# Turning the first group's input on the matrix engine: tails at once on column tiles, half loads, and the small first weights on ScalarE's queue

## The chip, the cores and the metric

The kernel runs on one core of a Trainium2 chip. The metric is the device time of one execution in microseconds (us). Times are medians of several executions. A "span" is the time from the first to the last instruction in one profiled execution; it is about 1.8 us shorter than the device time of the same execution. In the lines of the profile, PE stands for TensorE's matmuls and PEld for its weight loads, DVE for VectorE, ACT for ScalarE, POOL for GpSimd; SPq and ACTq are the issue of loads on SyncE's and on ScalarE's queue.

## The reference, cut to what matters

Six cross layers of a recommender network, 16384 rows of 416 features, bf16:

```python
B, F, D, L = 16384, 26, 16, 6          # Din = 416
def reference(x0, ws, bs):
    x = x0
    for l in range(L):
        proj = jnp.einsum('bd,de->be', x, ws[l]) + bs[l]
        x = x0 * proj + x
    return x
```

416 is 3 x 128 + 32. The last 32 features are the *tails*, and they are what makes the start of this kernel awkward.

## The kernel before: the parts that matter

The batch is cut into 8 groups of 2048 rows, and a group into 4 chunks of 512 rows. The kernel works on transposed data (features on partitions). Groups 1 and up are transposed by the DMA engines while they load. Group 0 cannot wait for that: its chunks are loaded as they are and turned on TensorE (a matmul against an identity matrix, into PSUM, the memory that matmuls write), then copied to SBUF (the memory that the engines work from) by ScalarE (ACT) and VectorE (DVE).

The program gives every engine a list of instructions of its own, in order. `add("sp", ...)` issues a DMA from SyncE, `add("act", ...)` with a `dma_start` issues one from ScalarE.

```python
# order of the loads on SyncE's queue
load_nat(0, 0, 2)                     # chunk 0, first half
load_nat(0, 2, KK)                    # chunk 0, second half
load_wm(0, "sp")                      # big weights of layer 0: 384 x 416
for j in range(1, NJ):
    load_nat(j, 0, KK)                # chunks 1, 2, 3
load_w3(0, "sp")                      # narrow weights of layer 0: 32 x 416, four copies
load_group(1, lambda: load_wm(1, "sp"))
# ... (cut)

def load_group(g, between=lambda: None):      # (cut)
    turn(0)                           # DMA-transposed load, features 0..127
    add("sp", lambda h: h.dma_start_transpose(Tb, x0[rows, D - P:D]), ...)   # last 128 features
    turn(1); turn(2)
    between()                         # big weights of layer 1
    for j in range(NJ):               # the group's tails: 32 rows out of Tb, to four places
        add("sp", lambda h: h.dma_start(x0s[s][q, XW:XW + CH], Tb[P - T32:P, j * CH:(j + 1) * CH]), ...)

def transposed_chunk(j):
    ba, bb = ((0, 1), (3, 0), (1, 3), (0, 1))[j]          # PSUM banks
    # ... (cut) 12 transposes of 128 x 128 for features 0..383 and
    #     4 more for features 288..415, of which only the last 32 are used;
    #     two ScalarE copies and two VectorE copies out of PSUM

def first_job():
    # ... (cut)
    keep_busy(8, 3)                   # dummy matmuls
    full(g, l, 0, ba, True, True, chunks=[0])             # 128-row matmuls, 3 a tile and chunk
    full(g, l, 1, bb, True, True, chunks=[0])
    transposed_chunk(1)
    transposed_chunk(2)
    full(g, l, 0, ba, True, True, chunks=[1])
    transposed_chunk(3)
    load_w3(1, "act")
    full(g, l, 1, bb, True, True, chunks=[1])
    full(g, l, 0, ba, True, True, chunks=[2, 3])
    rows32(g, l, 0, ba, False)        # the 32-row matmuls: tails times narrow weights
    # ... (cut)
```

**R0** is the start of the first 32-row matmuls (group 0). They need the tails and the *narrow weights*. **R1** is the start of the 32-row matmuls of group 1's first tile. They need *group 1's rows*, the four small moves at the end of `load_group`.

## Time and profile before

| | before |
|---|---|
| device time, 3 runs | 477.22 us (477.04 to 478.33) |
| profiled execution | 477.49 us, span 475.7 us |
| R0, R1 in that profile | 14.03, 22.78 us |

The page of the profile: busy time and share of the span of each engine, and further down the share of each engine in the chain of work that ended last.

```profile
PE 462.2 (97%) x3325; PEld 195.7 (41%) x3379; DVE 404.0 (85%) x696; ACT 342.4 (72%) x372; POOL 6.8 (1%) x15
...
PE 95%; issue 1%; DMA 1%; ACT 1%; DVE 1%; SPq 0%
```

TensorE is the limit: 95% of the last chain is PE. Next is the timeline of TensorE alone. Its columns are start, length (us), engine, source line, operation, output<-inputs, shapes, count, and in brackets how long the engine sat idle before and what ended that.

```profile
5.81 1.24 PE L456 MATMUL ps<-x,wm 128*128 128x512 bf16 x5 [0.25 <-ACT x L565]
7.92 1.07 PE L561 MATMUL ps<-ident,x 128*128 128x128 bf16 x16 [0.87 <-DMA x<-in_x_dram]
9.56 1.05 PE L561 MATMUL ps<-ident,x 128*128 128x128 bf16 x16 [0.57 <-DVE x L568]
10.45 0.81 PE L456 MATMUL ps<-x,wm 128*128 128x512 bf16 x3
11.10 1.06 PE L561 MATMUL ps<-ident,x 128*128 128x128 bf16 x16
12.21 1.89 PE L456 MATMUL ps<-x,wm 128*128 128x512 bf16 x8
14.03 0.40 PE L477 MATMUL ps<-x,w 32*128 32x512 bf16 x4
...
20.31 2.54 PE L456 MATMUL ps<-x,wm 128*128 128x512 bf16 x11 [0.16 <-issue]
22.78 0.61 PE L477 MATMUL ps<-x,w 32*128 32x512 bf16 x8
```

L456 are the 128-row matmuls, L561 the transposes, L477 the 32-row matmuls. TensorE waited for chunk 1 (0.87 us) and for chunk 2 (0.57 us; the profile names the VectorE copy, but chunk 2 landed at 9.42, at the same moment). A matmul record is missing here and there: six matmuls were issued in the first line and the first of them, at about 5.6, has no record. The ends of matmuls are modelled: counted at 216 ns from the start of the sixth (6.67), the gap before 7.92 is about 1 us.

SyncE's issue of loads, from the same timeline:

```profile
2.13 1.44 SPq L521 DMA_DIRECT2D x<-in_x_dram  x3
3.61 2.79 SPq L285 DMA_DIRECT2D w<-in_ws_dram  x4
6.44 4.11 SPq L292 DMA_TRANSPOSE x<-in_x_dram  x1
...
18.66 2.52 SPq L304 DMA_DIRECT2D x<-ost  x4
```

L285 are the four narrow weight loads, L292 and L297 the transposing loads of group 1, L304 the moves of its rows.

### The profile page before, as it was taken

The numbers are of one execution on the slowest core, as the hardware profiler recorded it, in microseconds if no ns is written. First come the engines' busy times: TensorE is split into PE (matmuls) and PEld (weight loads), VectorE is DVE, ScalarE is ACT, GpSimd is POOL, SyncE is SP. The second block draws the span as 40 slices with busy tenths as digits, with TensorE's granted clock in tenths as the row PEclk, the third lists the DMA queues.
The fourth block names the chain that finished last, engine by engine and source line by source line (L and its number), as shares of the span: only waits on it lengthen the run. The fifth ranks groups of instructions, "written<-read, shape, count | busy, mean of one in ns | idle before, by whom it ended". The sixth has DMA issues, their size and how long they took to land.

```text
span 475.7 us, 8355 instructions
## 1 busy us (share of the span) xinstructions
PE 462.2 (97%) x3325; PEld 195.7 (41%) x3379; DVE 404.0 (85%) x696; ACT 342.4 (72%) x372; POOL 6.8 (1%) x15
## 2 busy tenths in 40 slices
PE   7999999999999999999999999999999999999995
PEld 6344444444444444444444444434444444444442
DVE  2888888888888888898889869988888888888896
ACT  4677777777777777777777777777777777777785
POOL 1000000000000000000000000000000000000000
PEclk9999999999999999999999999999999999999999
DMA  8866950640002397369308940990000039025899
GB/s 223 181 150 137 190 113 1 142 81 1 28 7 44 63 228 158 76 139 244 84 21 195 208 108 9 178 279 2 1 10 25 4 64 242 15 45 117 227 155 288
DMA packets 138363, 53.31 MB, mean 112 GB/s; under 512 B 112330, under 2 KB 137428, under 8 KB 138324
## 3 DMA queue, kind: packets, MB, share of 16 engines
q1 hardware_dynamic: 137848, 52.46, 49.2%
q8 instruction: 26, 0.43, 0.4%
q10 hardware_dynamic: 476, 0.32, 0.2%
q14 instruction: 13, 0.11, 0.1%
HBM read 5.97 MB, written 13.63 MB: 41 GB/s over the span
## 4 chain that ended last, share of the span: by engine, by line
PE 95%; issue 1%; DMA 1%; ACT 1%; DVE 1%; SPq 0%
PE ps L456 77%; PE ps L477 7%; PE ps L497 6%; PE ps L798 2%; DMA x<-in_x_dram 1%; PE ps L471 1%; ACT tw L394 1%; PE ps L561 1%; PE ps L488 1%; DVE x L864 0%; PE ps L809 0%; ACT x L852 0%; DVE x L858 0%; PE ps L841 0%; SPq L521 0%
## 5 line engine op out<-in xcount | busy, mean ns | idle before, releaser
L394 ACT ACTIVATE tw<-ps,bias 128x1024 bf16<-128x1024 f32 (+1 forms) x295 | 299.8, 1071 | 119.8 <-PE ps L477 80.7
L456 PE MATMUL ps<-x,wm 128*128 128x512 bf16 x1638 | 371.7, 379 | 5.8 <-issue 3.7
L456 PEld LDWEIGHTS ps<-x,wm 128*128 128x128 bf16 x1692 | 158.9, 98 | 213.5 <-issue 27.9
L403 DVE TENSOR_TENSOR tw<-tw,x 128x1024 bf16<-128x1024 bf16 (+1 forms) x285 | 192.3, 682 | 52.8 <-ACT tw L394 52.4
L408 DVE TENSOR_TENSOR x<-tw,x 128x1024 bf16<-128x1024 bf16 (+1 forms) x285 | 183.0, 682 | 0.0
L477 PE MATMUL ps<-x,w 32*128 32x512 bf16 x512 | 39.2, 379 | 0.0
L497 PE MATMUL ps<-x,wm 128*32 128x512 bf16 x564 | 33.0, 380 | 0.0
L434 ACT ACTIVATE ts<-ps,bias 128x512 bf16<-128x512 f32 x47 | 28.8, 701 | 0.0
L438 DVE TENSOR_TENSOR x<-ts,x 128x512 bf16<-128x512 bf16 x47 | 18.6, 417 | 3.7 <-DMA x<-x 3.6
L497 PEld LDWEIGHTS ps<-x,wm 128*32 128x32 bf16 x564 | 13.8, 96 | 17.6 <-issue 5.3
L477 PEld LDWEIGHTS ps<-x,w 32*128 32x128 bf16 x512 | 7.8, 92 | 27.6 <-issue 27.1
L436 DVE TENSOR_TENSOR ts<-ts,x 128x512 bf16<-128x512 bf16 x47 | 18.5, 417 | 0.0
L666 POOL COPY ost<-ot 128x512 bf16<-128x512 bf16 x6 | 5.4, 898 | 423.7 <-DMA ot<-x 423.7
L798 PE MATMUL ps<-wm,x 128*128 128x416 bf16 x48 | 9.5, 340 | 0.0
L852 ACT ACTIVATE x<-ps 128x416 bf16<-128x416 f32 x16 | 7.7, 533 | 2.0 <-PE ps L798 1.9
L568 DVE COPY x<-ps 128x512 bf16<-128x512 bf16 x4 | 1.7, 424 | 8.7 <-PE ps L561 8.7
L565 ACT ACTIVATE x<-ps 128x512 bf16<-128x512 bf16 x8 | 4.3, 594 | 5.6 <-PE ps L561 5.6
L798 PEld LDWEIGHTS ps<-wm,x 128*128 128x128 bf16 x48 | 4.3, 98 | 4.2 <-issue 1.0
L561 PE MATMUL ps<-ident,x 128*128 128x128 bf16 x64 | 4.6, 226 | 1.4 <-DMA x<-in_x_dram 0.9
L858 DVE TENSOR_TENSOR x<-x,x 128x832 bf16<-128x832 bf16 (+1 forms) x10 | 5.0, 504 | 1.1 <-ACT x L852 1.1
L488 PE MATMUL ps<-x,w 32*32 32x512 bf16 x188 | 5.9, 374 | 0.0
L471 PE MATMUL ps<-x,w 32*32 32x512 bf16 x208 | 5.6, 385 | 0.0
(38 smaller groups left out, 35.7 us busy)
## 6 DMA issues: line engine op xcount, KB each, us to landing
out_dram<-ost SPq DMA_DIRECT2D x6, 1664.0 KB, 7.1
x<-in_x_dram SPq DMA_DIRECT2D x7, 416.0 KB, 8.0
x<-x SPq DMA_DIRECT2D x24, 96.0 KB, 2.2
wm<-in_ws_dram SPq DMA_DIRECT2D x6, 312.0 KB, 3.7
out_dram<-ost SPq DMA_DIRECT2D x2, 832.0 KB, 6.7
x<-x SPq DMA_DIRECT2D x22, 64.0 KB, 2.0
out_dram<-x SPq DMA_DIRECT2D x3, 416.0 KB, 3.6
x<-ost SPq DMA_DIRECT2D x28, 32.0 KB, 2.2
```

Of the source, the lines that this page charges most:

```text
L394: add("act", lambda h, a=a, w=w, b0=b0: h.activation(tw[r][:, a * CH:(a + w) * CH], psum[:, b0 * CH:(b0 + w) * CH], ACT_F.Identity, bias=b ...
L403: add("dve", lambda h, a=a, e=e: h.tensor_tensor(tw[r][:, a * CH:e * CH], tw[r][:, a * CH:e * CH], x0s[s0][:, i * GC + a * CH:i * GC + e * ...
L408: add("dve", lambda h, a=a, e=e: h.tensor_tensor(xs[so][:, i * GC + a * CH:i * GC + e * CH], tw[r][:, a * CH:e * CH], src(i, a, e), ALU.ad ...
L434: add("act", lambda h: h.activation(ts[r][:, :], bank(b), ACT_F.Identity, bias=bias[:, 3, l:l + 1], scale=1.0), reads=[("ps", b), "bias"], ...
L436: add("dve", lambda h: h.tensor_tensor(ts[r][:, :], ts[r][:, :], x03, ALU.mult), reads=[("ts", r)] + tok0, writes=[("ts", r)], release=True)
L438: add("dve", lambda h: h.tensor_tensor(x3s[so][:, :], ts[r][:, :], res, ALU.add), reads=[("ts", r)] + rtok, writes=[("x3", so), ("x3", so, ...
L456: add("pe", lambda h, t=t, j=j: h.matmul(bank(banks[j]), wm[l][:, t, ecols], src(t, j, j + 1), start=(first and t == 0), stop=(not first a ...
L471: add("pe", lambda h, q=q, j=j, r=r, c=c, o=o: h.matmul(psum[o, banks[j] * CH:(banks[j] + 1) * CH], w3[l][q, i * P + c * T32:i * P + (c + ...
L477: add("pe", lambda h, q=q, j=j, r=r: h.matmul(bank(banks[j]), w3[l][q, ecols], src[q, :], start=first, stop=not first, tile_position=(r * ...
L488: add("pe", lambda h, l=l, b=b, s3=s3, ri=ri, qi=qi, ro=ro, qo=qo: h.matmul(psum[qo, b * CH:(b + 1) * CH], w3[l][qi, NT * P:D], s3[qi, :], ...
L497: add("pe", lambda h, t=t, j=j, src=src, l=l, b=b, ro=ro, qo=qo: h.matmul(psum[qo, b * CH:(b + 1) * CH], wm[l][:, t, NT * P:D], src(t, j, ...
L798: add("pe", lambda h, t=t: h.matmul(bank(b, n=D), xcol(t, j, kk), wm[l][:, t, :], start=(first and t == 0), stop=(not first and t == NT - 1)),
```

## The change

The intent: turn all tails of group 0 at once, four side by side on column tiles of TensorE (strips of 128 x 32, each with a matmul of its own), instead of four full transposes in each chunk; load chunks 1 to 3 in halves so that the first half can be turned while the second is in flight; use separate pairs of PSUM banks; and take the four small narrow weight loads off SyncE's queue. The core of the diff:

```diff
     load_wm(0, "sp")
     for j in range(1, NJ):
-        load_nat(j, 0, KK)
-    load_w3(0, "sp")
+        load_nat(j, 0, 2)
+        load_nat(j, 2, KK)
     load_group(1, lambda: load_wm(1, "sp"))
@@ transposed_chunk
-        ba, bb = ((0, 1), (3, 0), (1, 3), (0, 1))[j]
+        ba, bb = ((0, 1), (3, 0), (6, 7), (0, 1))[j]
-        first = (0, P, 2 * P, D - P)
-        seq = [(t, k) for t in range(NT) for k in range(KK)]
         ... (cut)
-        q = slice(j * T32, (j + 1) * T32)
-        add("dve", lambda h: h.tensor_copy(x0s[s][q, XW:XW + CH], psum_t(bb)[P - T32:P, CH:2 * CH]),
-            reads=[("ps", bb)], writes=[("x03q", s, j)])
+        for k2 in (0, 2):                       # first half, then second half
+            for t in range(NT):
+                b, o = place[t]
+                for k in (k2, k2 + 1):
+                    ... (cut: one 128 x 128 transpose)
+    def transposed_tails(b):
+        for k in range(KK):
+            for j in range(NJ):
+                o = slice(j * T32, (j + 1) * T32)
+                add("pe", lambda h, j=j, k=k, o=o: h.matmul(
+                    psum_t(b)[o, CH + k * P:CH + (k + 1) * P], x0n[:, j, k, NT * P:D], ident[:, :],
+                    is_transpose=True, tile_position=(0, j * T32)), ... writes=[("ps", b)])
+        add("dve", lambda h: h.tensor_copy(x0s[s][:, XW:XW + CH], psum_t(b)[:, CH:2 * CH]), ...)
@@ first_job
-        keep_busy(8, 3)
+        load_w3(0, "act")
+        keep_busy(5, 3)
         full(g, l, 0, ba, True, True, chunks=[0])
         full(g, l, 1, bb, True, True, chunks=[0])
         transposed_chunk(1)
         transposed_chunk(2)
         full(g, l, 0, ba, True, True, chunks=[1])
+        full(g, l, 1, bb, True, True, chunks=[1])
         transposed_chunk(3)
+        transposed_tails(1)
         load_w3(1, "act")
-        full(g, l, 1, bb, True, True, chunks=[1])
         full(g, l, 0, ba, True, True, chunks=[2, 3])
```

More of the change, by code (lines that the diff above doesn't have):

```diff
@@ L549, in transposed_chunk @@
     def transposed_chunk(j):
-        ba, bb = ((0, 1), (3, 0), (1, 3), (0, 1))[j]
+        ba, bb = ((0, 1), (3, 0), (6, 7), (0, 1))[j]
         s = slot(0)
-        first = (0, P, 2 * P, D - P)
-        seq = [(t, k) for t in range(NT) for k in range(KK)]
-        if j == 0:
-            seq = [(t, k) for k2 in (0, 2) for t in range(NT) for k in (k2, k2 + 1)]
-        for n, (t, k) in enumerate(seq + [(NT, k) for k in range(KK)]):
-            if j == 0 and n == NT * 2:
-                keep_busy(2, 3)
-            b, o = (ba, t * CH) if t < 2 else (bb, (t - 2) * CH)
-            c = slice(o + k * P, o + (k + 1) * P)
-            add("pe", lambda h, t=t, k=k, b=b, c=c: h.transpose(
-                psum_t(b)[:, c], x0n[:, j, k, first[t]:first[t] + P], ident[:, :]),
-                reads=[("nat", j, k), x0_tok(nat, 0, 0), "ident"], writes=[("ps", b)])
@@ L564, in transposed_chunk @@
-        for t in range(2):
-            add("act", lambda h, t=t: h.activation(
-                x0s[s][:, cols(t, j)], psum_t(ba)[:, t * CH:(t + 1) * CH], ACT_F.Copy),
-                reads=[("ps", ba)], writes=[x0_tok(s, t, j)])
-        add("dve", lambda h: h.tensor_copy(x0s[s][:, cols(2, j)], psum_t(bb)[:, 0:CH]),
-            reads=[("ps", bb)], writes=[x0_tok(s, 2, j)])
-        q = slice(j * T32, (j + 1) * T32)
-        add("dve", lambda h: h.tensor_copy(x0s[s][q, XW:XW + CH], psum_t(bb)[P - T32:P, CH:2 * CH]),
-            reads=[("ps", bb)], writes=[("x03q", s, j)])
+        place = ((ba, 0), (bb, 0), (ba, CH)) if j == 0 else ((ba, 0), (ba, CH), (bb, 0))
@@ new lines, in transposed_chunk @@
+        for k2 in (0, 2):
+            for t in range(NT):
+                b, o = place[t]
+                for k in (k2, k2 + 1):
+                    c = slice(o + k * P, o + (k + 1) * P)
+                    add("pe", lambda h, t=t, k=k, b=b, c=c: h.transpose(
+                        psum_t(b)[:, c], x0n[:, j, k, t * P:(t + 1) * P], ident[:, :]),
+                        reads=[("nat", j, k), x0_tok(nat, 0, 0), "ident"], writes=[("ps", b)])
+            if j == 0 and k2 == 0:
+                keep_busy(2, 3)
@@ new lines, in transposed_chunk @@
+        for t in range(NT):
+            b, o = place[t]
+            dst, sp_ = x0s[s][:, cols(t, j)], psum_t(b)[:, o:o + CH]
+            kw = dict(reads=[("ps", b)], writes=[x0_tok(s, t, j)])
+            if b == bb:
+                add("dve", lambda h, dst=dst, sp_=sp_: h.tensor_copy(dst, sp_), **kw)
+            else:
+                add("act", lambda h, dst=dst, sp_=sp_: h.activation(dst, sp_, ACT_F.Copy), **kw)
+    def transposed_tails(b):
+        s = slot(0)
+        for k in range(KK):
[3 more added lines that the diff above has]
+                    psum_t(b)[o, CH + k * P:CH + (k + 1) * P], x0n[:, j, k, NT * P:D], ident[:, :],
+                    is_transpose=True, tile_position=(0, j * T32)),
+                    reads=[("nat", j, k), x0_tok(nat, 0, 0), "ident"], writes=[("ps", b)])
+        add("dve", lambda h: h.tensor_copy(x0s[s][:, XW:XW + CH], psum_t(b)[:, CH:2 * CH]),
+            reads=[("ps", b)], writes=x03_toks(s))
```

## The prediction

> **What bounds the kernel.** TensorE. The chain of waits puts 95% of the span on matmuls, and the granted clock is full. From 9.56 us to 460 us the timeline shows matmuls issued back to back (216 ns from one 512-column matmul to the next). Anything won before the first tile of group 1 (20.3 us) should therefore reach the end one for one, unless group 1's loads become the new limit. Only the first 20 us change.
>
> **The opening before** (timeline of TensorE, and landings of the loads): first matmuls of chunk 0 from 5.6 us, when the first weights land (5.46); idle 6.9 to 7.92, waiting for chunk 1 (landed 7.88); 16 transposes (56 ns each, 0.89 us); idle 8.83 to 9.56, waiting for chunk 2 (landed 9.42; the profile names the VectorE copy, which ends at the same time); 16 transposes; 3 matmuls; 16 transposes; 9 matmuls; the 32-row matmuls at 14.03. For chunks 1, 2 and 3, 15 of 16 DMA engines finish by 6.51, 7.55 and 8.77; one engine is 1.4 to 1.9 us late and sets the landing.
>
> **What the change does, costed.**
> 1. Each chunk loses 4 tail transposes: 16 x 56 ns = 0.89 us. But chunk 0's are hidden under the wait for the weights, and chunk 1's and part of 2's lie between DMA waits. About 0.4 us counts.
> 2. All tails as 16 column-tile transposes, four side by side. The Trainium skill ("TensorEngine Tiling (Array Packing)", Key Properties) says that tiles run in parallel and that a mode change drains TensorE; in this trace four column-tile matmuls start 3 ns apart and a mode change costs about 0.1 us. Estimate: 4 x 56 ns + 0.2 = 0.4 us added.
> 3. A new wait: the tails go into the bank that chunk 3's third block was just turned into, so they wait for its VectorE copy: 0.2 us to its start, 0.42 us copy, 0.1 us back: about 0.7 us of TensorE idle right before the tails. Before, chunk 3's copies hid behind matmuls.
> 4. Half loads: first halves turn before the second halves land; after each landing 6 transposes (0.33 us) remain instead of 16 (0.89). This wins about 0.5 us after chunk 1 and again about as much after chunk 2, but the second only replaces the first where the late engine still sets chunk 2's landing.
> 5. Four narrow weight loads leave SyncE's queue (2.8 us of issue), three more chunk loads join (1.4 us): group 1's transposing loads are issued about 1.4 us earlier, but queue behind the same chunk bytes. ScalarE now issues the four (about 1.7 to 2.6 us from 5.6 us), which may delay its copies of chunk 1 until about 8.2 us.
> 6. Bank 3 no longer joins chunks 1 and 2: nothing measurable. VectorE saves three 0.43 us copies: off the path.
>
> **Sum.** If one engine is late again: -0.5 (halves) -0.4 + 0.4 (tails) + 0.7 (bank wait) = about +0.2 us. If it is not: both DMA idles (1.7 us) mostly vanish, less ScalarE's issue delay: about -1 us. Weighted: -0.5 us.
>
> Predicted **476.7 us**, range **475.6 to 477.8**. Chances: faster by over 2% 0.003, within 2% 0.992, slower by over 2% 0.005.
>
> **Right or wrong in the profile:** chunk 2's transposes follow chunk 1's with a gap under 0.4 us; 48 full transposes; 16 tail transposes within 0.5 us; a TensorE gap of 0.6 to 0.8 us just before them, ended by the VectorE copy; first 32-row matmuls between 12.9 and 14.4 us (before 14.03); from there the same stream, shifted by a constant.
>
> **What would make it wrong:** ScalarE's issue of the weights blocking its copies longer than 2.6 us; group 1's rows landing late (21.97 before, used at 22.77), capping the gain; the late engine moving.

## More of the kernel before

When a load has landed is read from its completions, 16 for each load: the trace has the time of each of them. The narrow weights (64 completions) had landed at 11.18 us, long before R0. Group 1's rows (64 completions) had landed at 22.53, a quarter of a microsecond before R1.

## The result

Ratios here and below are the mean time of one kernel's fast runs over the mean of the other's fast runs of the same rounds, so they are not quite the ratio of the medians that are quoted.

| | before | changed |
|---|---|---|
| device time | 477.31 us (476.76 to 478.33, 6 runs) | 477.80 us (477.39 to 478.82, 6 runs) |
| ratio | | 1.0011, 95% interval 0.9996 to 1.0026 |
| span of the profiled execution | 475.69 us | 476.40 us |
| R0, R1 | 14.03, 22.78 us | 14.76, 23.51 us |
| narrow weights landed | 11.18 us | 14.62 us |
| group 1's rows landed | 22.53 us | 23.15 us |

The interval reaches from just below 1 upward: the same within 2%, and no gain. The page of the profile after, the same lines:

```profile
PE 462.5 (97%) x3322; PEld 195.7 (41%) x3376; DVE 402.0 (84%) x693; ACT 342.1 (72%) x372; POOL 7.3 (2%) x15
...
PE 94%; DMA 2%; ACT 1%; issue 1%; DVE 1%; ACTq 0%; POOL 0%; POOLq 0%
```

The timeline of TensorE after, as shown for before (L558 are now the full transposes, L578 the tails on column tiles):

```profile
5.87 1.72 PE L456 MATMUL ps<-x,wm 128*128 128x512 bf16 x5
7.42 1.17 PE L558 MATMUL ps<-ident,x 128*128 128x128 bf16 x18
8.84 0.51 PE L558 MATMUL ps<-ident,x 128*128 128x128 bf16 x6 [0.25 <-DMA x<-in_x_dram]
9.19 1.46 PE L456 MATMUL ps<-x,wm 128*128 128x512 bf16 x6
10.48 0.83 PE L558 MATMUL ps<-ident,x 128*128 128x128 bf16 x12
11.83 0.41 PE L578 MATMUL ps<-ident,x 128*32 128x128 bf16 x16 [0.52 <-DVE x L568]
12.40 1.24 PE L456 MATMUL ps<-x,wm 128*128 128x512 bf16 x5 [0.16 <-ACT x L570]
14.76 0.40 PE L477 MATMUL ps<-x,w 32*128 32x512 bf16 x4 [1.11 <-DMA w<-in_ws_dram]
...
21.04 2.54 PE L456 MATMUL ps<-x,wm 128*128 128x512 bf16 x11 [0.16 <-issue]
23.51 0.61 PE L477 MATMUL ps<-x,w 32*128 32x512 bf16 x8
```

Nearly everything that was intended happened. The transposes of chunks 1 and 2 follow each other, with 0.25 us of idle before the last six. The 16 tail transposes take 0.41 us. The last 128-row matmul before R0 started at 13.26, and in the kernel before the step from there to the 32-row matmuls was 0.31 us: R0 could have been at 13.58, that is 0.45 us *earlier* than before. Then TensorE waited. R0 came at 14.76, and the releaser is `DMA w<-in_ws_dram`: the narrow weights. In the chain of waits after, this is one piece, which starts with the last of the four loads' issue and ends at 14.62 (start, length, what):

```profile
6.70 7.92 DMA w<-in_ws_dram
```

And SyncE's issue after:

```profile
2.45 2.86 SPq L521 DMA_DIRECT2D x<-in_x_dram  x6
5.35 4.52 SPq L292 DMA_TRANSPOSE x<-in_x_dram  x1
...
19.39 2.51 SPq L304 DMA_DIRECT2D x<-ost  x4
```

Group 1's first transposing load is issued 1.1 us earlier (5.35, before 6.44). Yet it landed later: 14.82 us against 13.81. Its issue alone took 4.52 us.

### The profile page after: what moved, and what is told of

The parts are those of the page before. It is cut to its first block, busy times and chain, and to the rows that moved or that the text cites. A ratio compares the mean times of both kernels' runs of the same rounds, so it can differ in the third digit from the quotient of the medians.

```text
span 476.4 us, 8347 instructions
## 1 busy us (share of the span) xinstructions
PE 462.5 (97%) x3322; PEld 195.7 (41%) x3376; DVE 402.0 (84%) x693; ACT 342.1 (72%) x372; POOL 7.3 (2%) x15
## 4 chain that ended last, share of the span: by engine, by line
PE 94%; DMA 2%; ACT 1%; issue 1%; DVE 1%; ACTq 0%; POOL 0%; POOLq 0%
PE ps L456 76%; PE ps L477 7%; PE ps L497 6%; DMA w<-in_ws_dram 2%; PE ps L811 2%; PE ps L471 1%; ACT tw L394 1%; PE ps L541 1%; PE ps L488 1%; DVE x L877 0%; PE ps L558 0%; PE ps L822 0%; ACT x L865 0%; ACT x L570 0%; DVE x L871 0%
## 5 line engine op out<-in xcount | busy, mean ns | idle before, releaser
L877 DVE TENSOR_TENSOR x<-x,x 128x832 bf16<-128x832 bf16 x8 | 4.6, 586 | 0.4 <-DMA x<-x 0.4
```

## The experiments

Seventeen runs were made, some of them of the same kernel on another occasion. All gave correct results. Each was timed in five rounds beside the kernel before. This table has for each profiled execution what the argument needs; it is worked out from the traces (landing: the last of 64 completions).

| run | narrow weights landed | R0 | rows landed | R1 | span | span - R1 |
|---|---|---|---|---|---|---|
| before | 11.18 | 14.03 | 22.53 | 22.78 | 475.69 | 452.91 |
| changed | 14.62 | 14.76 | 23.15 | 23.51 | 476.40 | 452.89 |
| w3_on_sync | 10.47 | 13.21 | 21.95 | 22.00 | 474.90 | 452.90 |
| w3_early_scalar | 6.61 | 16.19 | 22.46 | 24.94 | 477.83 | 452.89 |
| before_w3_scalar | 14.94 | 15.08 | 23.77 | 23.83 | 476.75 | 452.92 |
| whole_chunks | 14.45 | 14.58 | 23.17 | 23.33 | 476.24 | 452.90 |
| tails_bank7 | 13.96 | 14.01 | 22.33 | 22.76 | 475.66 | 452.90 |
| w3_sync_bank7 | 11.14 | 12.77 | 22.31 | 22.35 | 475.25 | 452.90 |
| w3_sync_whole_chunks | 11.21 | 14.26 | 22.41 | 23.01 | 476.07 | 453.06 |
| group1_rows_early | 10.94 | 12.58 | 21.35 | 21.40 | 474.30 | 452.90 |
| before_rows_early | 10.44 | 13.26 | 20.84 | 22.01 | 474.92 | 452.91 |
| w3_early_kept_busy | 6.83 | 14.85 | 21.76 | 23.60 | 476.50 | 452.90 |
| group1_rows_again | 11.27 | 13.67 | 21.98 | 22.42 | 475.33 | 452.91 |
| transposes_wait_w3 | 9.95 | 13.25 | 23.75 | 23.80 | 476.70 | 452.90 |
| changed_again | 14.15 | 14.29 | 23.01 | 23.06 | 475.96 | 452.90 |
| w3_on_sync_again | 11.25 | 13.58 | 22.95 | 23.00 | 475.99 | 452.99 |
| fastest_third | 11.28 | 12.65 | 21.91 | 21.95 | 474.85 | 452.90 |
| rows_early_w3_scalar | 14.26 | 14.30 | 21.98 | 23.05 | 475.94 | 452.89 |

Read the last column first. From R1 to the end every profiled execution took 452.9 us, within 0.2 us. So the whole case is decided by when R1 starts, and R1 starts when two things have come: TensorE has got there (8.75 us after R0, where nothing stops it), and group 1's rows have landed. The missing run, rows_early_only, had its profile in a throttled execution and is told below.

The theories. **Queue theory**: what cost is the wait for the narrow weights, which sit in ScalarE's queue and share the DMA engines with group 1's transposing loads. Rivals: the **halves theory** (twice as many chunk loads make everything behind them late), the **bank theory** (the wait before the tails, which the prediction had counted), and later the **limit theory** (group 1's rows).

### w3_on_sync

```diff
-        load_w3(0, "act")                 # in first_job
+    load_w3(0, "sp")                      # after the chunk loads, before load_group(1)
```

> The changed kernel with one part undone: the four narrow weight loads are issued by SyncE again, after the chunk loads and before group 1's transposing loads. Queue theory (the 1.1 us wait before the first 32-row matmuls exists because these loads sit in ScalarE's queue and share the DMA engines with group 1's transposing loads): they land before 11.8 us, the wait is gone, the first 32-row matmul starts at 13.5 to 13.8 us instead of 14.76, and the time is 0.2 to 0.5 us below the kernel before (about 1 us below the changed kernel), unless group 1's rows then land too late and cap it. Halves theory (twice as many chunk loads stretch the loading, so whatever is queued behind lands late): a wait of over 0.5 us stays before the 32-row matmuls and the time stays 0.3 us or more above the kernel before.

Measured: 477.35 us (476.71 to 477.66, 5 runs); before 477.14 us (476.71 to 477.98, 11 runs); ratio 1.0001, 0.9989 to 1.0013. The weights landed at 10.47, the wait was gone, and R0 came at 13.21. The profiled execution was also the fastest of the five. The median did not fall below the kernel before, so the expected time was missed. The queue theory was right about the wait, but something else stood behind it: the rows landed at 21.95 and were used at 22.00, with nothing to spare.

### w3_early_scalar

```diff
+    load_w3(0, "act")                     # before the loads of chunk 0
     load_nat(0, 0, 2)
@@ first_job
-        load_w3(0, "act")
```

> The changed kernel with the narrow weight loads still on ScalarE's queue, but issued right after ScalarE's first dummy activation (about 2.8 us) instead of about 5.4 us. Queue theory, sharpened: not the queue itself is at fault but sharing the engines with the transposing loads; issued early they land before 8.5 us, the first 32-row matmul starts at 13.5 to 14.0 us and the time is 0.1 to 0.6 us below the kernel before. If ScalarE's queue as such is slow: they land after 12 us again and the wait stays.

Measured: 477.65 us (476.73 to 479.64, 6 runs); before as above; ratio 1.0016, 0.9998 to 1.0033. The issue began at 1.4 us rather than at 2.8. The weights landed at 6.61, so ScalarE's queue is not slow as such. But the big first weights then landed at 7.01 (5.73 in the changed kernel), and something new happened. The timeline of TensorE shows six matmuls that took 2.70 us:

```profile
7.15 2.70 PE L456 MATMUL ps<-x,wm 128*128 128x512 bf16 x6 [1.82 <-DMA wm<-in_ws_dram]
```

and the window from 7.0 to 9.6 us (columns: window, its length, then busy time and count of PE, PEld, DVE, ACT and POOL, then the granted TensorE clock, the DMA share and GB/s) has a granted clock of 0.54:

```profile
7.00:9.60 2.60, 2.45 (x6) 0.89 (x7) 0.00 (x0) 0.00 (x0) 0.00 (x0) 0.54 1.41 291
```

The trace's own record has the full clock from 3.79 to 7.21 and half of it from 7.21 to 10.62. The halving followed 1.8 us of idle (5.33 to 7.15), and matmuls came every 427 ns instead of 216. That is one profile. The six runs, from 476.73 to 479.64, spread by 2.9 us. As a test of the queue theory the time of this run is inconclusive.

### before_w3_scalar

```diff
-    load_w3(0, "sp")                      # the kernel before, with this one part of the change
@@ first_job
+        load_w3(0, "act")
         keep_busy(8, 3)
```

> The kernel before with this one part of the change: the narrow first weights on ScalarE's queue. Queue theory: they land at 13.5 to 15 us, the first 32-row matmul (14.03 before) waits for them and starts at 14.3 to 15.2 us; time 0.3 to 1.1 us above the kernel before. Halves theory: whole chunk loads leave room, the weights land before 13 us and the time equals the kernel before within 0.2 us.

Measured: 478.25 us (477.71 to 479.03, 5 runs); before 477.14 us; ratio 1.0021, 1.0008 to 1.0034. This one part, alone, makes the kernel before slower. The timeline of TensorE in this run shows the same wait as in the changed kernel, with whole chunk loads and without the tails' change:

```profile
11.96 2.10 PE L456 MATMUL ps<-x,wm 128*128 128x512 bf16 x9
15.08 0.40 PE L477 MATMUL ps<-x,w 32*128 32x512 bf16 x4 [1.01 <-DMA w<-in_ws_dram]
```

The halves theory fell here.

### whole_chunks

```diff
     for j in range(1, NJ):
-        load_nat(j, 0, 2)
-        load_nat(j, 2, KK)
+        load_nat(j, 0, KK)
```

> The changed kernel with whole chunk loads (three loads instead of six), all else changed. Queue theory: the wait for the narrow weights stays (first 32-row matmul after 14.4 us), time 0.3 to 1.0 us above the kernel before; the idle between the transposes of chunks 1 and 2 grows because each chunk is waited for whole. Halves theory: the weights land before 13 us, no wait over 0.3 us, and the time is at or below the kernel before.

Measured: 477.70 us (477.33 to 478.21, 5 runs); ratio 1.0012, 1.0000 to 1.0024. The narrow weights landed at 14.45 and R0 was at 14.58: with or without halves, the weights set R0.

### tails_bank7

```diff
-        transposed_tails(1)
+        transposed_tails(7)
```

> The changed kernel with the tails turned into bank 7 instead of bank 1, so that they need not wait for the VectorE copy out of bank 1. My prediction called that wait 0.7 us of loss (the trace after shows 0.5 us of idle). If the narrow weights' landing is what ends last before the 32-row matmuls (queue theory), the 0.5 us only moves into the wait for them: the idle before the tails falls under 0.2 us, the wait before the first 32-row matmul grows from 1.1 to about 1.6 us, that matmul still starts after 14.4 us and the time stays within 0.2 us of the changed kernel. Bank theory (the bank wait eats the gain): the time falls by 0.4 to 0.6 us against the changed kernel, to about the kernel before.

Measured: 477.61 us (477.20 to 478.23, 5 runs); before 477.21 us (476.54 to 477.45, 9 runs); ratio 1.0014, 1.0001 to 1.0026. The wait before the tails was gone and the time did not move against the changed kernel (477.80). R0 was released by the weights at 13.96. They landed 0.66 us earlier than in the changed kernel's profile, so two expected numbers were missed: R0 came at 14.01, not after 14.4, and the wait for the weights did not grow. The bank wait was real, but it was not what set R0, so the bank theory fell.

### w3_sync_bank7

```diff
-        load_w3(0, "act")
+    load_w3(0, "sp")                      # as in w3_on_sync
-        transposed_tails(1)
+        transposed_tails(7)
```

> Narrow weights on SyncE again and the tails in bank 7. The first 32-row matmul starts about 0.5 us earlier than with the weights on SyncE alone (13.2 in that profile), at about 12.7. Limit theory (group 1's rows, which landed at 21.95 and were used at 22.00 there, are the next limit): TensorE then waits 0.3 to 0.6 us for those rows before the 32-row matmuls of group 1's first tile, and the time falls by at most 0.2 us, to 0.1 to 0.5 us below the kernel before. Without that limit: the whole 0.5 us arrives.

Measured: 477.19 us (477.00 to 477.39, 5 runs); before 477.21 us; ratio 1.0004, 0.9990 to 1.0018. R0 came at 12.77, 1.26 us earlier than in the profile before. R1 came only 0.42 us earlier. TensorE's timeline shows where the rest stayed:

```profile
12.77 0.40 PE L477 MATMUL ps<-x,w 32*128 32x512 bf16 x4
...
22.35 0.61 PE L477 MATMUL ps<-x,w 32*128 32x512 bf16 x8 [0.64 <-DMA x<-ost]
```

The 32-row matmuls of group 1 waited for `DMA x<-ost`, the rows, which landed at 22.31. This is the limit theory as expected, only that the time didn't even fall to 0.1 us below the kernel before.

### w3_sync_whole_chunks

```diff
     load_wm(0, "sp")
     for j in range(1, NJ):
-        load_nat(j, 0, 2)
-        load_nat(j, 2, KK)
+        load_nat(j, 0, KK)                # with w3_on_sync's edit
```

> Narrow weights on SyncE again, whole chunk loads: what the halves alone are worth. If they pay as predicted (about 0.5 us per chunk waited for), the idle between chunk 1's and chunk 2's transposes comes back at 0.5 us or more and the time is 0.3 to 0.6 us above the version with halves. If halves only add packets and issues: equal or up to 0.3 us faster.

Measured: 477.61 us (476.75 to 478.06, 5 runs); before 477.21 us; ratio 1.0011, 0.9998 to 1.0024. TensorE idled again before chunk 1's transposes (0.2 us) and before chunk 2's (0.3 us), less than the expected 0.5. R0 was at 14.26, later than in either run of w3_on_sync (13.21 and 13.58). In time no value of the halves is shown: the ratio lies between those of the two runs of w3_on_sync (1.0001 and 1.0015).

### group1_rows_early, group1_rows_again and fastest_third

One kernel, run on three occasions. On top of w3_sync_bank7, group 1's rows are moved ahead of the big weights of layer 1, and the narrow weights of layer 1 go to SyncE after them, so that nothing shares the engines with the transposing loads:

```diff
         turn(2)
-        between()
         for j in range(NJ):
             ...                           # the four moves of the rows
+        between()
@@
-    load_group(1, lambda: load_wm(1, "sp"))
+    load_group(1, lambda: (load_wm(1, "sp"), load_w3(1, "sp")))
@@ first_job
-        load_w3(1, "act")
```

> As the version with weights on SyncE and tails in bank 7, and group 1's four row moves issued before the second big weight load, and the second narrow weights on SyncE after them instead of on ScalarE's queue, so that nothing shares the engines with group 1's transposing loads. Limit theory: group 1's rows land 1 us or more earlier (before 21 us), TensorE does not wait for them, and the time is 0.5 to 1.2 us below the kernel before. If it stays at the kernel before within 0.2 us, the limit lies elsewhere.

> The fastest version once more, for a second sample on another occasion: 0.5 to 1.2 us below the kernel before, ratio 0.9975 to 0.999.

> The fastest version a third time (first narrow weights on SyncE, tails in bank 7, group 1's row moves ahead, second narrow weights on SyncE): its two samples gave 0.9988 and 1.0000 of the kernel before. If it is really faster: 0.2 to 0.9 us below the kernel before. If the first sample was luck: within 0.15 us of it. In the profile TensorE waits neither for the narrow weights nor for group 1's rows.

| occasion | this kernel | before, same rounds | ratio |
|---|---|---|---|
| group1_rows_early | 476.32 us (475.99 to 476.99, 5 runs) | 477.21 us | 0.9988, 0.9975 to 1.0000 |
| group1_rows_again | 476.96 us (476.04 to 478.54, 6 runs) | 477.04 us | 1.0000, 0.9988 to 1.0012 |
| fastest_third | 476.67 us (476.59 to 476.96, 5 runs) | 476.97 us | 0.9996, 0.9982 to 1.0009 |

Its median was the lower one each time, by 0.89, 0.08 and 0.30 us, but two of three intervals hold 1 well inside and the third ends at it. The mean of the three ratios, 0.9995, would be about a quarter of a microsecond, and even that is not proven. In the first profile the rows landed at 21.35, not before 21 as expected, and were used at once. In the second profile the big first weights landed at 6.72 (5.44 in the first), which differs between executions of the same kernel; R0 was 1.09 us later too (13.67 against 12.58). In the third, R0 was at 12.65, the earliest but one, and the rows stopped TensorE once more, at 21.91:

```profile
12.65 0.39 PE L477 MATMUL ps<-x,w 32*128 32x512 bf16 x4
...
18.70 2.77 PE L456 MATMUL ps<-x,wm 128*128 128x512 bf16 x12
21.95 0.61 PE L477 MATMUL ps<-x,w 32*128 32x512 bf16 x8 [0.49 <-DMA x<-ost]
```

### rows_early_only

```diff
         turn(2)
-        between()
         ...
+        between()                         # with w3_sync_bank7's edits; w3 of layer 1 stays on ScalarE
```

> Weights on SyncE, tails in bank 7, group 1's row moves ahead of the second big weight load, but the second narrow weights still on ScalarE's queue beside group 1's transposing loads. If the order of the row moves alone lifted the limit: rows land before 21.8 us, at most 0.3 us of wait for them, time 0.4 to 0.9 us below the kernel before. If sharing with the second narrow weights also costs: transposing loads end 0.3 to 0.7 us later than in the fastest version and its time is 0.2 to 0.5 us above that one.

Measured: four fast runs between 476.92 and 477.38; before 477.04 us; ratio 1.0002, 0.9989 to 1.0015. The profile fell in an execution of 607.19 us with a granted clock of 0.754, so its times can't be compared with the others. That misses the expected 0.4 to 0.9 us below, but the full version in the same rounds (group1_rows_again, 1.0000) can't be told from it either. What moving the second narrow weights adds is not shown.

### before_rows_early

The kernel before with the edits of group1_rows_early to `load_group(1)` and `load_w3(1)`, and nothing of the change.

> The kernel before, with group 1's four row moves ahead of the second big weight load and the second narrow weights on SyncE: the last two steps of the fastest version so far, without anything of the change. If the change's own parts (halves, tails at once) are what was won there, once the two waits were taken away: TensorE reaches the 32-row matmuls at about 14 us as before, group 1's rows landing earlier is worth nothing there, and the time is within 0.3 us of the kernel before. If the gain came from group 1's loads alone: 0.6 to 1 us below it.

Measured: 477.18 us (476.72 to 477.32, 5 runs); before 477.04 us; ratio 1.0003, 0.9990 to 1.0016. The rows landed at 20.84 and were used at 22.01, so 1.2 us were to spare, and the time did not move. As long as the opening is the old one, early rows are worth nothing.

### w3_early_kept_busy

```diff
+    load_w3(0, "act")                     # early, as in w3_early_scalar
-        keep_busy(5, 3)
+        keep_busy(30, 3)
```

> The changed kernel with the narrow weights early on ScalarE's queue, as before, and 30 instead of 5 dummy matmuls while waiting for the big first weights, so that TensorE doesn't sit idle for 2 us. In the first try its clock was granted at half (a 512-column matmul every 427 ns) after that idle. If the idle caused it: all matmuls come at 216 ns, the slow runs (478 to 479.6) are gone, and the median lies between 476.6 and 477.4. If not, the spread of 3 us stays.

Measured: 478.14 us (477.54 to 478.57, 5 runs); before 477.04 us; ratio 1.0023, 1.0011 to 1.0035. The 512-column matmuls came at 216 ns, and the spread fell from 2.9 to 1.0 us, which fits idle as the cause of the halved clock. The median was wrong: the big weights landed at 6.23, but 30 dummy matmuls kept TensorE until 7.47, which is a loss of my own making. The profile is no clean counterpart of the first one: its clock record begins with the full clock only at 6.43, and the dummies before it came every 107 ns, those after it every 56.

### transposes_wait_w3

The narrow weights stay on ScalarE's queue. Group 1's first transposing load waits for their semaphore. For this the group's load is written after them in the program; the order on each engine's own queue stays the same.

```diff
         load_w3(0, "act")
+        load_group(1, lambda: load_wm(1, "sp"))      # moved here, SyncE's order is unchanged
@@ load_group, turn(0)
+                reads=[("w3", 0, j) for j in range(NJ)] if g == 1 and t == 0 else [],
```

> The changed kernel with the narrow weights on ScalarE's queue at the same moment as in it, but group 1's first transposing load waits until they have landed. Sharing theory (what makes them late is that their packets take turns with the transposing loads' packets): they land before 11 us, the wait before the first 32-row matmuls is under 0.2 us and these start at 13.2 to 13.9 us; group 1's loads then start later and its rows may land after 22.5 us, so part of the gain is given back there. Late-queue theory (issued at 5.4 us on ScalarE's queue behind 1.25 MB of chunk loads they are late in any case): they still land after 13 us and the wait stays.

Measured: 478.74 us (478.37 to 479.16, 5 runs); before 476.80 us (476.57 to 477.74, 9 runs); ratio 1.0037, 1.0023 to 1.0050. The weights, issued from 4.87 on the same queue, landed at 9.95 instead of 14.62, and R0 came at 13.25 without a wait. So it is the sharing with the transposing loads, not the queue, that makes them late. But the transposing loads now began at 9.96, and TensorE's timeline shows the price in group 1:

```profile
11.85 1.47 PE L457 MATMUL ps<-x,wm 128*128 128x512 bf16 x6
13.25 0.40 PE L478 MATMUL ps<-x,w 32*128 32x512 bf16 x4
...
21.68 1.04 PE L457 MATMUL ps<-x,wm 128*128 128x512 bf16 x4 [0.47 <-DMA x<-in_x_dram]
23.80 0.40 PE L478 MATMUL ps<-x,w 32*128 32x512 bf16 x4 [1.09 <-DMA x<-ost]
```

Both of group 1's late loads stop TensorE, the third block of features (L457) and then the rows (L478), which landed at 23.75.

### changed_again and w3_on_sync_again

The changed kernel and w3_on_sync, unaltered, in the same rounds.

> The changed kernel unaltered, beside the next run on the same chip. First 32-row matmul again at 14.0 to 15.1 us, released by the narrow weights; time 0.3 to 0.7 us above the kernel before.

> The changed kernel with the narrow weights on SyncE, once more, beside the changed kernel. Queue theory: 0.3 to 0.8 us faster than the changed kernel, within 0.2 us of the kernel before, no wait for the narrow weights in the profile (first 32-row matmul between 13.2 and 14.2 us, depending on when the chunks land). If its time equals the changed kernel's within 0.15 us, the wait is not what cost.

Measured: changed 477.60 us (477.51 to 477.85, 5 runs), ratio 1.0013, 1.0000 to 1.0025; w3_on_sync 477.71 us (477.25 to 478.63, 5 runs), ratio 1.0015, 1.0003 to 1.0028; before 476.80 us. The expectation of the second was missed. R0 was released by the weights in one (landed 14.15, R0 14.29) and came without a wait in the other (13.58), yet R1 was the same, 23.06 and 23.00. In w3_on_sync_again the timeline of TensorE says why:

```profile
13.58 0.40 PE L477 MATMUL ps<-x,w 32*128 32x512 bf16 x4
...
19.63 2.77 PE L456 MATMUL ps<-x,wm 128*128 128x512 bf16 x12
23.00 0.61 PE L477 MATMUL ps<-x,w 32*128 32x512 bf16 x8 [0.60 <-DMA x<-ost]
```

The rows landed at 22.95 here (21.95 in the first run of this kernel). Without the wait for the weights TensorE simply waits at the next place. So the queue theory alone does not explain the time: there are two limits, one behind the other.

### rows_early_w3_scalar

The kernel of group1_rows_early with one thing put back: `load_w3(0, "act")` as in the change.

> The same version with one thing put back as the change has it: the first narrow weights on ScalarE's queue. Two-limits theory (they cost twice, by their own late landing and by slowing group 1's transposing loads): they land after 13 us, the first 32-row matmul starts after 13.8 us instead of about 13, and the time is 0.4 to 1.2 us above the version with them on SyncE, about 0.2 to 0.7 us above the kernel before. If group 1's rows were the only limit: with the rows moved ahead the time equals the version on SyncE within 0.2 us.

Measured: 477.63 us (477.29 to 478.22, 5 runs) against 476.67 us (476.59 to 476.96) for the same kernel with the weights on SyncE, in the same rounds; the ranges don't touch. Ratio to before 1.0015, 1.0002 to 1.0028. With the rows out of the way (landed 21.98, needed at 23.05), the narrow weights are the limit again and cost about 1 us:

```profile
11.78 1.50 PE L456 MATMUL ps<-x,wm 128*128 128x512 bf16 x6
14.30 0.40 PE L477 MATMUL ps<-x,w 32*128 32x512 bf16 x4 [1.03 <-DMA w<-in_ws_dram]
...
23.05 0.61 PE L477 MATMUL ps<-x,w 32*128 32x512 bf16 x8
```

## Why the prediction was wrong, point by point

The prediction said 476.7 us, half a microsecond below the kernel before. Measured was 477.80, at the edge of its range, half a microsecond above (medians, 477.80 - 477.31 = 0.49).

**What held.** The kernel's time does follow the opening one for one (span - R1 is constant). The tails cost about what was estimated: 0.41 us for 16 transposes, and their starts lie in 0.19 us, groups of four at 3 to 5 ns from one to the next. The Trainium skill, "TensorEngine Tiling (Array Packing)", Key Properties, says that tiles work in parallel and that a change of mode drains TensorE. This trace agrees with the first, and on the second shows a step of 0.31 us from a 128-row matmul to the 32-row ones instead of the usual 0.216. The bank wait was there, 0.52 us of idle instead of 0.7. The halves closed most of the gap between chunks 1 and 2 (0.25 us of idle was left). ScalarE's issue of the weights took 2.0 us (5.36 to 7.34) and did not delay its copies of chunk 1, which began at 8.18, after their transposes. No DMA engine was as late on chunk 1 as in the profile before (last completion 6.91, before 7.88).

**The step that failed is step 5**, with the term it fed into the sum, "less ScalarE's issue delay". The prediction asked what the issue of the four loads would hold up on ScalarE, and took their landing for granted, because they were small and R0 was far. They are 104 KB in all. Beside group 1's transposing loads they took from 5.36 to 14.62 us. The Trainium skill states the mechanism ("DMA: Bandwidth & Descriptors", Queues, rings and completion order): SyncE and ScalarE each own a row of rings on the same 16 DMA engines, and each engine goes round robin between the rows that have work. The trace of the changed kernel agrees as far as it goes: in each microsecond from 8 to 13 ScalarE's queue moved packets (54, 15, 58, 46, 19) beside SyncE's (499, 319, 687, 629, 596); whose turn came when on one engine was not read. The prediction cited nothing of this. While the weights were on SyncE's queue they stood ahead of the transposing loads and landed at 10.4 to 11.3 us in every profile; on ScalarE's queue at that moment they took turns with them and landed at 13.96 to 14.94 in all six profiles. The later issue is not what did it: in w3_on_sync they were issued from 5.40, as late as in the changed kernel, and landed at 10.47. transposes_wait_w3 shows it from the other side. This turned 0.45 us of gain at R0 into 0.73 us of loss: 1.18 us of waiting.

**A pause of the loads is part of that wait.** In all six of those profiles the weights' completions stop for 1.2 to 1.7 us, and the last 8 to 19 of the 64 come after it. In the changed kernel 56 had come by 12.75 us, before R0 could have started; the other eight came from 14.27 to 14.62. On SyncE's queue all 64 had come before such a pause. So sharing made the weights late enough to be caught by it; how much they would have cost without it no run shows. The pause itself is taken up under "What stays open".

**The second failure is a number that was misread.** The prediction wrote "21.97 before, used at 22.77" for group 1's rows and so saw 0.8 us of room. By 22.00 us only 42 of the 64 completions had come. The last one was at 22.53, so the room was 0.25 us. Group 1's rows were named as something that could cap the gain, but with the right number they would have stood in the sum: no faster opening could have won more than a quarter of a microsecond unless the rows came earlier too. And step 5 expected group 1's loads 1.4 us earlier in issue with no harm; they were issued 1.1 us earlier, and the rows landed 0.6 us later. For the first transposing load the harm shows in every profile: beside the shared weights it landed at 14.18 to 15.15, with them on SyncE at 12.79 to 13.90. For the rows the ranges overlap (22.33 to 23.77 against 21.95 to 22.95 where their order was the old one), so that sharing delays the rows too is not shown.

**What the two together explain.** Each wait hides the other. Take the weights off the shared path and the rows stop TensorE (w3_on_sync_again). Move the rows ahead and the weights stop it (rows_early_w3_scalar). Ease both, with the tails in bank 7, and the median came lowest of all kernels in its rounds, each time, though by as little as 0.08 us.

**The starting point was a poor draw too.** The profile before had one DMA engine 1.4 to 1.9 us late on chunks 1 to 3. In before_rows_early, whose opening is the same, no engine was late and R0 was at 13.26 instead of 14.03. The gaps that the halves were to close are in part the luck of one execution. So the 0.45 us is a gain over that execution only: with the weights on SyncE the changed kernel had R0 at 13.21 and 13.58, no better than 13.26, and only the tails in bank 7 brought it to 12.58 to 12.77 (13.67 where the big weights landed at 6.72). The later runs of the kernel before, in five sets of rounds, have median spans of 475.0 to 475.4 us; less the 452.9 us from the table, their R1 was at about 22.1 to 22.5 (an estimate), not at 22.78. What made that engine late was not tried.

Of the prediction's two cases the one without a late engine came, for which it had about -1 us. Even without the wait for the weights it would have been -0.45: TensorE went on after chunk 2's landing at 8.84 instead of 9.56, 0.72 us earlier, and gave back 0.27 on the way to R0, where the bank wait (0.52) now stands.

**What stays open.** Late in the opening the DMA engines nearly stand still. The windows of the changed kernel from 13 to 15 us (columns as before; the last is GB/s):

```profile
13.00:14.00 1.00, 0.64 (x3) 0.10 (x1) 0.00 (x0) 0.00 (x0) 0.00 (x0) 1.00 0.05 5
14.00:15.00 1.00, 0.24 (x4) 0.13 (x4) 0.00 (x0) 0.00 (x0) 0.00 (x0) 1.00 0.96 217
```

5 GB/s in the microsecond from 13 to 14, and eight of the 64 completions of the narrow weights came only after it. At that time one 16,384-byte packet of the instruction queue ran, from 12.07, for 1.43 us. In the profile before such a packet ran from 12.05 for 0.96 us. The kept traces say more: each of the 18 profiles in the table has one such packet here, starting between 10.19 and 13.99. In transposes_wait_w3 no load was in flight beside it. In the other 17 the half microsecond with the fewest bytes between 8 and 17 us (31 GB/s or less) lies around or just after that packet's end. The pause moves with the packet, whichever queue the weights are on. No run moved the packet on purpose, so that it causes the pause is not shown.

## What to carry to other kernels

A small load that is needed soon should not be moved to another engine's queue only to free the first queue's issue time: on the other queue it no longer stands ahead of the bulk, and takes turns with it (about 1 us in rows_early_w3_scalar). Before you cost a faster opening, look for the next thing that TensorE will need, and read its *last* completion against the moment of use; the smaller of the gain and that distance is what you can win. When a wait is removed and the time doesn't move, look at the next place where the same engine waits before you doubt the first.

## What the Trainium skill lacked or had wrong

- "DMA: Bandwidth & Descriptors" says that queues share the engines, but not how much a load suffers beside a DMA transpose: four loads of 26 KB took 9.3 us from first issue to last landing (5.36 to 14.62), and 5.1 us (4.87 to 9.95) with the transposes held back. The transpose beside them landed at 14.82 instead of 13.81.
- The same page has nothing on a near standstill of all engines while transposes are in flight: 5 GB/s from 13 to 14 us in the changed kernel, 81 GB/s in the same window of the kernel before, each around or just after the end of a 16 KB instruction packet (13.49 and 13.01).
- "TensorE: Matmul & The Clock Gate", What's actually happening, gives an idle window of about 3.4 us before the clock is halved. In w3_early_scalar the clock was halved after a stretch of 3.41 us (3.79 to 7.21) of which TensorE idled only the last 1.8: matmuls at 427 ns, granted clock 0.54 from 7.0 to 9.6 us. That is one execution. In group1_rows_again a shorter idle of about 1.2 us left it at full speed.
- "TensorEngine Tiling (Array Packing)" gives no time for the drain at a change of mode: here the step from a 128-row matmul to 32-row ones is 0.31 us instead of 0.216.
